# Natural row order and a new planned order in an adaLN, linear-attention and MLP kernel

## The chip, the cores and the metric

The kernel runs on one core of a Trainium2 chip. Its time is the device time of one execution in microseconds (us), and less is better. The core has TensorE (PE, matrix products; PEld is its weight loads), VectorE (DVE), ScalarE (ACT), GpSimd (POOL) and SyncE (SP). Each engine works off its own instructions in a fixed order and waits for the others by semaphores. In this part of the kernel all transfers are issued by SP, so SP's queue is also the queue of the transfers.

## What is computed (reference, cut)

```python
def _A_ref(x, wqkv, wo):                 # H = 32 heads of 18
    qkv = ...(x @ wqkv)...               # q, k, v
    phi = lambda t: jnp.where(t > 0, t + 1, jnp.exp(t)) + 1e-6
    pq, pk = phi(q), phi(k)
    kv = jnp.einsum("bhsd,bhse->bhde", pk, v)
    z = jnp.einsum("bhsd->bhd", pk)
    num = jnp.einsum("bhqd,bhde->bhqe", pq, kv)
    den = jnp.einsum("bhqd,bhd->bhq", pq, z)[..., None] + 1e-6
    return ...(num / den)... @ wo

def _B_ref(x, w1, w2):
    return _silu(x @ w1) @ w2

mod = (_silu(c) @ w_mod).reshape(c.shape[0], 6, 1, -1)
sa, ca, ga, sb, cb, gb = (mod[:, 0], ..., mod[:, 5])
h = _layernorm(x) * (1 + ca) + sa
x = x + ga * _A_ref(h, A_wqkv, A_wo)
h = _layernorm(x) * (1 + cb) + sb
x = x + gb * _B_ref(h, B_w1, B_w2)
```

x has 2048 rows (tokens) of 576; wqkv is 576 x 1728, w1 576 x 4608, w2 4608 x 576, w_mod 576 x 3456. All are float32.

## The kernel before, in words

**Tiles.** The rows are handled as 16 tiles of 128 (t = 0 to 15), four of them to a block (b = 0 to 3). `acc[t]` in `accb[b]` holds a tile's results. A float32 operand of a matmul is split into a high and a low part, and a product takes three passes, so each split is an ACT copy (high) and a DVE or POOL subtraction (low).

**Stages.** Up to about 35 us block 0 and the weights are started, in an order written by hand. From about 30 to 250 us runs the *planned stage*: k for tiles 2 to 15 and q for tiles 0 to 10 (L851), the sums of x against phi(k) (L971), the product with the v weights (L1099), and with Wo (L1136). After it come attention and the first MLP groups (to about 400 us), the MLP (L1826 up, L1910 down) and the last plain group (L1943), whose output is added by `plain_add` (L1948) and stored by `plain_store` (L1954).

**The planned stage's order.** `pe(...)` and `do(...)` enter steps with an engine, an assumed duration, what they read and write, and a lag (how long after a transfer is issued its data are assumed to land). `Schedule.emit` works out for each step the latest start (`late`) that does not delay PE's fixed order, then walks through time: each engine takes, of the steps that are ready, the one with the smallest `late`. The result is the fixed order on every engine, SP's queue included. A static order of this kind that assumes a landing too early puts a waiting instruction in front of others that could run.

**A block's turn.** `early_steps(b)` loads the block's four tiles into `accb[3]` (`row4`, L916), takes their statistics (DVE L242, L243) and works out mean and deviation (L923 DVE, L924 POOL, L925 DVE). `block_steps(b)` normalises (L257 ACT, L259 DVE), transposes 32 x 32 pieces on DVE (L936), stores them to DRAM (`turned`, L942) and fetches them back turned (L948, and the tail L953). `turn_steps(b)` modulates the fetched chunks (L265, L267) and splits them into `hT` (L907 ACT, L908 DVE), which PE's products with the k and q weights read. `dealt` and `taken` are views that reorder the columns as they are written to `hT`, so that column t*128 + p belongs to partition p of tile t.

**Row order before.** For t >= 4, `pieces` says where a tile's rows lie: partition 32a + j of tile t of a block holds row 128a + 32t + j. A load of a tile, of a block, or a store of a result is therefore four transfers of 32 partitions each (L916, L723, L1933, L1954).

**Projected tiles.** `phi_steps` takes exp on ACT (L857), the maximum on DVE (L862), and their combination on DVE (L407). A PSUM bank of the two (`K0`, `K1`) is free once exp and maximum have read it. `k_steps` then splits the tile (L872 ACT, L875 DVE or POOL) and adds it to `zsum` (POOL L876).

**Modulation sums and first scan.** `mod_steps(piece)` makes two of the six modulation vectors each: five loads of w_mod (L347) into two rooms, `raw2`, scaled on ACT (L1012, L1014), added on POOL (L1015), the partial sums written to DRAM (`parts`, L1016), read back in another order in 36-byte runs (L1019), reduced on DVE (L1022) and written out as a vector (L1023). Before, piece 1 stands in block 0 and piece 2 in block 1. `bound_steps` and `first_scan`/`factor_first` take maxima and sums of squares from which the MLP's scale factors come; they stand at the end of the stage. `load_late` loads Wo and the v weights and multiplies Wo by the gate (L1088, DVE).

Of the kernel before, what the change touches and what calls it, by code (L numbers as in the profile page):

```python
# [24 lines left out]
def kernel(ctx: ExitStack, tc, A_x, A_wqkv, A_wo, B_x, B_w1, B_w2, c, w_mod, out):  # L25
# [33 lines left out]
    def behind(instructions):  # L59

        with ExitStack() as order:
# [31 lines left out]
            2-4 0-1 6-13 5 14-25 28-31 26-27 32-43 50-53 47 45 44 46 55-62 49 54 48 63-66 68 67 70-71 69 74 83  # L93
            73 75-76 72 77-81 84-85 87 86 82
# [235 lines left out]

    def pieces(t, n=1):
        if t < 4:
            return [(slice(0, P), lambda y: y[t * P : (t + n) * P].rearrange("(u p) d -> p u d", u=n))]
        r0 = [t // 4 * 512 + a * P + t % 4 * 32 for a in range(4)]
        return [(slice(32 * a, 32 * a + 32), lambda y, r=r: y[r : r + 32 * n].rearrange("(u j) d -> j u d", u=n))
                for a, r in enumerate(r0)]
# [387 lines left out]

    def q_norm(t, prod, pn):
# [10 lines left out]
        load_rows_of(a, t)  # L736
        return pn

    class Schedule:
# [4 lines left out]
        def __init__(self):  # L744
            self.ops, self.wrote, self.seen, self.order = [], {}, {}, []

        def add(self, eng, us, emit, reads=(), writes=(), lag=0.0, tensor=None):
# [8 lines left out]
            self.ops.append((eng, us, emit, lag, need))  # L756
            if eng == "PE":
                self.order.append((tensor, i))

        def emit(self):  # L760
# [18 lines left out]
            turn = 0  # L779
            for _ in range(n):  # L780
# [8 lines left out]
                i = min((i for i in some if ready[i] <= at_), key=lambda i: (late[i], i))  # L789
                open_[e].remove(i)  # L790
# [24 lines left out]
    plan = Schedule()  # L815
# [8 lines left out]
    def do(eng, us, emit, reads=(), writes=(), lag=0.0):  # L824
        plan.add(eng, us, emit, reads, writes, lag)
# [39 lines left out]
    BY_ACT = ()  # L865
# [12 lines left out]
    def q_steps(t):  # L878
        ps, k = project(t, wqp_)
        phi_steps(ps, k, acc[t], [f"acc{t}", *ACC.get(t, ())])  # L880

    def split_rows():

        C = KC * P
        for t in range(4):
            do("ACT", 0.68, lambda t=t: A.copy(xs[t][:, :D], xt[:, t, :D]), [f"xt{t}"], [f"xhi{t}"])
            eng, us = (V, 0.74) if t < 2 else (G, 1.55)
            do("DVE" if t < 2 else "POOL", us, lambda t=t, eng=eng: eng.tensor_sub(xs[t][:, DX:], xt[:, t, :C], f32(xs[t][:, :C])),
# [9 lines left out]
    def turn_steps(b):  # L898

        for k in START:  # L900
# [3 lines left out]
            eng, us = (V, 0.69) if k in (1, 3) else (A, 0.81)  # L904
            do("DVE" if k in (1, 3) else "ACT", us, lambda src=src, chunk=chunk, eng=eng: modulate(src, *chunk[1:], eng), [], [name])
# [4 lines left out]
    def early_steps(b):  # L910
# [16 lines left out]
    def block_steps(b):  # L927

        row4 = accb[NB - 1]
        for t in range(4):  # L930
            eng, us = (A, 0.87) if t % 2 else (V, 0.7)
            do("ACT" if t % 2 else "DVE", us, lambda t=t, eng=eng: ln.normalise(t, xt[:, t], row4[:, t], eng, ((0, 0, D),)),
# [67 lines left out]
    raws2 = [[f"raw{i}.{a}" for a in range(2)] for i in range(2)]  # L1000
    of_raw = count()

    def mod_steps(piece):
        parts, vec = parts_of[piece - 1], vec_of[piece - 1]
        for k in START:
            kp, i = P if k < KC else 64, next(of_raw) % 2
            raw, dst = raw2[i], tmod2[:kp, :, 0:D]
            kp = raw.shape[0] if k < KC else 64
            do("SP", 0.1, lambda raw=raw, k=k: load_mod(raw, piece, k), [], raws2[i], 8.0)
            scale = sc[:kp, k : k + 1]  # L1010
            if k == 0:
                do("ACT", 1.25, lambda raw=raw, dst=dst, kp=kp, scale=scale: A.activation(dst, raw[:kp], AF.Identity, scale=scale), raws2[i], ["tmod"])  # L1012
            else:
                do("ACT", 1.25, lambda raw=raw, kp=kp, scale=scale: A.activation(raw[:kp], raw[:kp], AF.Identity, scale=scale), [], raws2[i])  # L1014
                do("POOL", 2.7, lambda raw=raw, dst=dst, kp=kp: G.tensor_add(dst, dst, raw[:kp]), raws2[i], ["tmod"])  # L1015
        do("SP", 0.1, lambda: nc.sync.dma_start(parts, tmod2[:, :, 0:D]), ["tmod"], [f"parts{piece}"], 5.5)  # L1016
# [3 lines left out]
           [f"parts{piece}"], raws2[i], 8.0)  # L1020
# [3 lines left out]
           [f"s9{piece}"], [f"vec{piece}"], 5.0)  # L1024
# [12 lines left out]
    first_spots = [r[:, i : i + n] for r in (sq, xT) for i, n in ((0, 1024), (1024, 1024), (2048, 256))]  # L1037

    def first_scan():
        parts, *n = scans(0, first_spots, 1024)  # L1040
        rooms = [SQ[0:2], SQ[2:3], SQ[3:4], XT[0:2], XT[2:4], ["xT4"]]
        for (load, square), room in zip(parts, rooms):
            do("SP", 0.1, load, [], room, 8.0)
# [1271 lines left out]
```

## Time and profile before

| | us |
|---|---|
| median of 3 runs | 1146.26 (1145.07 to 1146.29) |
| the profiled execution | 1145.7 |
| its span, first to last instruction | 1144.0 |
| mean granted TensorE clock | 0.976 of full speed |

| engine | busy us | share of the span |
|---|---|---|
| PE | 1081.1 | 95% |
| DVE | 927.1 | 81% |
| POOL | 722.1 | 63% |
| ACT | 695.5 | 61% |

Two views carry most of what follows. The busy time by stretch gives, for a piece of the span, how long each engine worked and at which clock PE ran. The timeline of an engine gives each instruction, or a run of equal ones, with its start and duration; in brackets behind it stand the idle time before it and what ended that. Rows named SPq are issues of transfers: their duration is that of the issue. The time from issue to landing stands in the view of the transfers, as the last number of a row.

### The profile page before, as it was taken

The page shows a single profiled execution, that of the slowest core. Times are in us where ns is not written, and L with a number is a line of the kernel's source. Part 1 is how long each engine was busy: PE and PEld are TensorE (multiplying, and loading weights), DVE is VectorE, ACT ScalarE, POOL GpSimd, SP SyncE. Part 2 cuts the span into 40 slices and gives each one's busy share as a digit, 9 for nine tenths or more (in the row PEclk, how much of TensorE's full clock was granted, in tenths as well). Part 3 has the DMA queues.
Part 4 walks back from the last instruction along what each step waited for, and adds up shares of the span by engine and source line. Part 5 has one row for each costly group of instructions (what it writes and reads, how often), then busy time and mean ns, then how long its engine had stood idle before and what let it go on. Part 6 is the DMA issues. An engine that isn't in the chain of part 4 may idle for free.

```text
span 1144.0 us, 19228 instructions
## 1 busy us (share of the span) xinstructions
PE 1081.1 (95%) x7027; PEld 773.8 (68%) x7027; DVE 927.1 (81%) x1467; ACT 695.5 (61%) x1300; POOL 722.1 (63%) x789
## 2 busy tenths in 40 slices
PE   8878797999999997999999999999999999999995
PEld 7878797899888544566666666666666666666664
DVE  7858494968699888989898888897897887898765
ACT  4653334333855668767777677686686586675562
POOL 2435162335462468977978868878778778777462
PEclk9988898899999999999999999999999999999998
DMA  9268629514333575767756757747748738626523
GB/s 287 60 160 100 154 68 144 152 54 110 120 85 129 207 230 164 268 165 235 218 182 219 213 171 241 228 135 253 230 117 256 235 111 272 200 78 196 163 72 83
DMA packets 121071, 193.52 MB, mean 169 GB/s; under 512 B 44492, under 2 KB 79312, under 8 KB 120976
## 3 DMA queue, kind: packets, MB, share of 16 engines
q1 hardware_dynamic: 120804, 192.00, 58.1%
q8 instruction: 55, 0.90, 0.3%
q10 hardware_dynamic: 172, 0.30, 0.1%
q14 instruction: 40, 0.33, 0.1%
HBM read 176.77 MB, written 15.48 MB: 168 GB/s over the span
## 4 chain that ended last, share of the span: by engine, by line
PE 73%; DVE 9%; DMA 7%; POOL 4%; ACT 3%; issue 2%; SPq 1%; DVEq 0%; POOLq 0%; ACTq 0%
PE up L1826 28%; PE down L1910 28%; PE big L295 7%; PE psK L851 3%; DMA acc<-turned 2%; PE small L1334 1%; PE psG L971 1%; DMA turned<-acc 1%; PE big L1345 1%; DMA raw<-parts 1%; DVE xt L259 1%; PE psK L1136 1%; DVE acc L936 1%; DVE a L407 1%; PE big L1259 1%
## 5 line engine op out<-in xcount | busy, mean ns | idle before, releaser
L1826 PE MATMUL up<-hT,w 128*128 128x512 f16 x1264 | 317.0, 380 | 8.2 <-DMA hT<-hd 3.2
L1826 PEld LDWEIGHTS <-w 128*128 128x128 f16 x1492 | 146.0, 98 | 142.5 <-issue 10.0
L1919 DVE SCALAR_TENSOR_TENSOR acc<-acc,set,down 128x576 f32<-128x576 f32 x128 | 103.5, 810 | 34.8 <-PE down L1910 33.9
L1864 POOL TENSOR_TENSOR s<-f,f 128x256 f32<-128x256 f32 x66 | 54.7, 830 | 92.5 <-ACT f L1845 90.2
L1844 ACT ACTIVATE f<-f,set 128x512 f32<-128x512 f32 x102 | 73.3, 719 | 61.5 <-DVE f L1850 51.6
L1910 PE MATMUL down<-w,hb 128*128 128x288 f16 x600 | 88.9, 286 | 2.5 <-DVE U L1921 1.7
L1910 PE MATMUL down<-w,hc 128*128 128x288 f16 x600 | 88.9, 286 | 0.2 <-DVE acc L1923 0.2
L1910 PE MATMUL down<-w,hT 128*128 128x288 f16 x480 | 82.9, 286 | 0.4 <-DVE acc L1923 0.4
L1848 DVE TENSOR_TENSOR f<-up,p 128x512 f32<-128x512 f32 x102 | 69.5, 682 | 13.0 <-PE up L1826 7.6
L1845 ACT ACTIVATE f<-f,set 128x512 f32<-128x512 f32 x102 | 73.6, 722 | 3.3
L1910 PEld LDWEIGHTS <-hb 128*128 128x128 f16 x600 | 58.7, 98 | 24.6 <-issue 2.8
L851 PE MATMUL psK<-w,hT 128*128 128x288 f32 x308 | 54.5, 330 | 20.4 <-DVE hT L908 9.2
L1910 PEld LDWEIGHTS <-hc 128*128 128x128 f16 x600 | 58.7, 98 | 21.9 <-issue 0.5
L1850 DVE TENSOR_TENSOR f<-up,f 128x512 f32<-128x512 f32 x68 | 46.8, 688 | 24.5 <-PE up L1826 23.8
L1888 POOL TENSOR_TENSOR hc<-s,hc 128x512 f16<-128x512 f32 x50 | 62.8, 1255 | 5.6 <-ACT hc L1884 5.6
L1910 PEld LDWEIGHTS <-hT 128*128 128x128 f16 x480 | 46.9, 98 | 26.7 <-issue 0.8
L851 PEld LDWEIGHTS psK<-w,hT 128*128 128x128 f32 x308 | 49.6, 218 | 22.5 <-DVE hT L908 10.5
L1868 POOL TENSOR_TENSOR f<-f,s 128x256 f32<-128x256 f32 x66 | 53.6, 812 | 16.5 <-DVE hb L1888 9.4
L1861 POOL TENSOR_TENSOR s<-f 128x256 f32<-128x256 f32 x66 | 56.3, 852 | 7.0 <-ACT f L1841 4.8
L1866 POOL TENSOR_TENSOR s<-s,f 128x256 f32<-128x256 f32 x66 | 56.9, 863 | 3.4
L1910 PE MATMUL down<-w,hd 128*128 128x288 f16 x396 | 54.9, 288 | 0.0
L1910 PE MATMUL down<-w,ha 128*128 128x288 f16 x396 | 54.4, 286 | 0.1
(398 smaller groups left out, 2807.4 us busy)
## 6 DMA issues: line engine op xcount, KB each, us to landing
hT<-hd SPq DMA_DIRECT2D x101, 640.0 KB, 5.0
hT<-hd SPq DMA_DIRECT2D x65, 512.0 KB, 3.9
hT<-in_B_w_dram SPq DMA_DIRECT2D x14, 576.0 KB, 4.7
hT<-in_B_w_dram SPq DMA_DIRECT2D x28, 256.0 KB, 5.6
raw<-in_B_w_dram SPq DMA_DIRECT2D x9, 576.0 KB, 6.4
v<-in_B_w_dram SPq DMA_DIRECT2D x9, 576.0 KB, 5.2
acc<-in_A_x_dram SPq DMA_DIRECT2D x16, 288.0 KB, 6.3
raw<-in_w_mod_dram SPq DMA_DIRECT2D x8, 576.0 KB, 5.0
```

The source lines that it names most:

```text
L295: T.matmul(ps, xpart(a), wpart(b), start=n == 0, stop=n == len(XW) - 1)
L851: T.matmul(o, part(a), w(b), start=c == 0 and m == 0, stop=c == KC and m == 1)
L1826: T.matmul(ps, left, right, start=first and m == 0, stop=m == len(seq) - 1, skip_group_check=True)
L1844: A.activation(f, f, AF.Silu, scale=factor(self.g, "inv"))
L1845: aside(A.activation(f, f, AF.Identity, scale=factor(self.g, "delta")))
L1848: V.tensor_add(f, self.bank[bank[1]], self.p1)
L1861: G.tensor_sub(self.s3, half(i, 0, 0), half(i, 0, 1))
L1864: G.tensor_add(self.s[:, 0:1], half(i, 0, 1), half(i, 1, 1))
L1866: G.tensor_sub(self.s[:, 1:2], self.s[:, 0:1], half(i, 0, 0))
L1888: eng.tensor_sub(t[:, :, 1, :], src, t[:, :, 0, :])
L1910: T.matmul(ps[:, p, :HALF], left[:, u, p * P : (p + 1) * P], right[:, v], start=n in (1, 5, 7, 6) and j == 0, stop=j == len(passes) - 1, s ...
L1919: V.scalar_tensor_tensor(dst, dst, factor(self.g, "ratio"), ps[:, :, :HALF], op0=ALU.mult, op1=ALU.add)
```

## The change

**Row order.** `pieces` and `load_rows_of` are gone: partition p of tile t holds row 128t + p everywhere. Each load of a tile or a block and each store is one transfer over 128 partitions. `dealt` and `taken` stay as they are. The hand-written order of SP behind the planned stage is the same one, renumbered for the smaller number of transfers.

**The planner.** `add` takes a `due` time, by which a step should have been done; it enters `late`. With `ahead`, an engine other than PE and SP may leave the step that it would take, and wait for a more urgent one that becomes ready before that step would end. The second planned stage (the MLP) keeps the plain rule.

**Assumed landings.** Block loads 7 to 9, store 5.2 to 6, fetches 5 and 6 to 6 and 7, w_mod loads 8 to 9, `parts` write 5.5 to 8 and read 8 to 14, scan loads 8 to 14.

**Work moved.** `mod_steps(2)`, the gate's row, `bound_steps`, `first_scan` and `factor_first` are entered right behind `mod_steps(1)`, in block 0, with due times. w_mod is loaded into four rooms (two of them in `accb[1]`), and the POOL addition is split into two halves. The scan uses `raw2` in pieces of 1152 columns, and `z` for its broadcast; the mask is made ahead of the last `split_rows`. The maximum of the k tiles goes from DVE to ACT (`BY_ACT = range(4)`: Relu and a bias pass). Wo is loaded into `raw2` and `xt[0]`, and its gate multiplication goes from DVE to POOL.

```diff
-    def load_rows_of(a, t):
-        for p, rows in pieces(t):
-            nc.sync.dma_start(a[p], rows(x)[:, 0])
...
-        load_rows_of(a, t)
+        nc.sync.dma_start(a, x[t * P : (t + 1) * P, :])
...
-        def emit(self):
+        def emit(self, ahead=False):
...
-                late[i] = min(begin.get(i, t + 8.0), end - lag - us)
+                late[i] = min(begin.get(i, t + 8.0), self.due[i] - us, end - lag - us)
...
+                if ahead and e not in ("PE", "SP"):
+                    end = at_ + ops[i][1]
+                    urgent = [j for j in some if ready[j] < end and late[j] < min(late[i], end - shift)]
+                    i = min(urgent, key=lambda j: (late[j], j), default=i)
+                    at_ = max(at_, ready[i])
+                if e == "PE":
+                    shift = max(shift, at_ - begin[i])
...
-    BY_ACT = ()
+    BY_ACT, Q_ACT, NORM_V, TURN_V, XS_V, WO_V = range(4), (), (0, 2), (1, 3), (0, 1), False
...
-        def load():
-            for p, rows in pieces(4 * b, 4):
-                nc.sync.dma_start(row4[p], rows(x))
-
-        do("SP", 0.3, load, [], SQ, 7.0)
+        rows = x[b * 512 : (b + 1) * 512, :].rearrange("(t p) d -> p t d", p=P)
+        do("SP", 0.1, lambda: nc.sync.dma_start(row4, rows), [], SQ, 9.0)
...
-        do("SP", 0.4, store, SQ, [f"turned{b}"], 5.2)
-        do("SP", 0.4, fetch_main, [f"turned{b}"], XT, 5.0)
-        do("SP", 0.4, fetch_tail, [f"turned{b}"], [XTAIL], 6.0)
+        do("SP", 0.4, store, SQ, [f"turned{b}"], 6.0)
+        do("SP", 0.4, fetch_main, [f"turned{b}"], XT, 6.0)
+        do("SP", 0.4, fetch_tail, [f"turned{b}"], [XTAIL], 7.0)
...
+    mod_rooms = [accb[1][:, 0:2], accb[1][:, 2:4], *raw2]
+    mod_names = [["acc4", "acc5"], ["acc6", "acc7"], *raws2]
...
-                do("POOL", 2.7, lambda raw=raw, dst=dst, kp=kp: G.tensor_add(dst, dst, raw[:kp]), raws2[i], ["tmod"])
+                for a in range(2):
+                    do("POOL", 1.45, lambda raw=raw, dst=dst, a=a: G.tensor_add(dst[:, a], dst[:, a], raw[:, a]), [names[a]], [f"tmod{a}"])
...
-           [f"parts{piece}"], raws2[i], 8.0)
+           [f"parts{piece}"], raws2[i], 14.0)
...
+            do("ACT", 1.35, lambda square=square: square(found), [], [*room, "found"], due=140.0)
...
-            do("DVE", 1.1, lambda cc=cc, n=n: V.tensor_mul(wos[cc][:n], wos[cc][:n], bc["ga"][:n]), ["bcga"], [wo_names[cc]])
+            do("DVE" if WO_V else "POOL", 1.1 if WO_V else 1.5, lambda cc=cc, n=n: (V if WO_V else G).tensor_mul(wos[cc][:n], wos[cc][:n], bc["ga"][:n]), ["bcga"], [wo_names[cc]])
...
     mod_steps(1)
+    mod_steps(2)
+    do("SP", 0.1, lambda: mod_row("ga", vec_of[0][0]), ["vec1"], ["bcga"], 5.0)
+    bound_steps()
+    steps = first_scan()
+    factor_first(steps)
     q_steps(2)
...
-        plan.emit()
+        plan.emit(AHEAD)
...
         def store(self, b, i, k):
-            for p, rows in pieces(4 * b + 2 * i, 2):
-                nc.sync.dma_start(rows(of[:, k * HALF : (k + 1) * HALF]), self.c(b, i, k)[p])
+            t0 = (4 * b + 2 * i) * P
+            dst = of[t0 : t0 + 2 * P, k * HALF : (k + 1) * HALF]
+            nc.sync.dma_start(dst.rearrange("(i p) d -> p i d", p=P), self.c(b, i, k))
...
-            for p, rows in pieces(a):
-                nc.sync.dma_start(rows(of[:, c])[:, 0], acc[a][p, c])
+            nc.sync.dma_start(of[a * P : (a + 1) * P, c], acc[a][:, c])
```

More of the change, by code (lines that the diff above doesn't have):

```diff
@@ L1057, in bound_steps @@
         do("DVE", 0.75, lambda: find_limit(2, bc["gb"]), ["bcgb"], ["limits"])
-        do("DVE", 1.6, find_bounds, [], ["limits", "colb", "bounds"])
+        do("DVE", 1.6, find_bounds, [], ["limits", "colb", "bounds"], due=140.0)
     def factor_first(steps):
@@ L1076, in rest @@
             V.tensor_scalar(bc["gb"], bc["gb"], factor(0, "gamma"), None, op0=ALU.mult)
-        do("DVE", 2.0, rest, [], ["small", "bcgb"])
-    wos = [xt[:, i, :D] for i in range(4)] + [raw2[1][:, 0, :]]
-    wo_names = [f"xt{i}" for i in range(4)] + ["raw1.0"]
-    wvs = [acc[12 + i] for i in range(4)] + [raw2[1][:, 1, :]]
+        do("DVE", 2.0, rest, [], ["small", "bcgb"], due=175.0)
+    wos = [raw2[i // 2][:, i % 2] for i in range(4)] + [xt[:, 0, :D]]
+    wo_names = [*raws2[0], *raws2[1], "xt0"]
+    wvs = [acc[12 + i] for i in range(4)] + [xt[:, 1, :D]]
     def load_late():
@@ L1223 @@
     z_steps()
-    do("POOL", 1.2, lambda: G.memset(kvm, 0.0), [], ["tmod", "kvm"])
+    do("POOL", 1.2, lambda: G.memset(kvm, 0.0), [], ["tmod0", "tmod1", "kvm"])
     for c in (2, 3, 4):
```

86 lines of the change are left out of this document (38 added, 48 removed).

## The prediction

> **What bounds the kernel now.** I began with the busy time of each engine by stage (start and end of a stretch in us, its length, then busy us and instruction count of PE, PEld, DVE, ACT and POOL, the granted TensorE clock, the DMA share, GB/s).
>
> ```profile
> 30.00:250.00 220.00, 188.59 (x1253) 181.69 (x1254) 160.44 (x247) 87.36 (x140) 82.47 (x57) 0.90 0.56 113
> 250.00:400.00 150.00, 146.48 (x1055) 125.02 (x1056) 126.51 (x230) 88.52 (x148) 75.32 (x71) 1.00 0.41 126
> 400.00:1100.00 700.00, 688.45 (x4338) 424.41 (x4336) 592.35 (x899) 486.73 (x960) 537.70 (x634) 1.00 0.63 197
> 1100.00:1144.00 44.00, 32.41 (x226) 21.88 (x224) 25.71 (x40) 17.65 (x27) 19.13 (x17) 0.93 0.29 75
> ```
>
> From 250 to 1100 TensorE is busy for 834.93 of 850 us at full clock, and the edits there concern only row loads that no PE wait names. So the change is worth what it does in two places: the planned stage (30 to 250 us: 31.4 us of PE idle, clock 0.90) and the end.
>
> In the planned stage I read PE's waits next (waiter, released by: us in total, times, longest), then the stretches around them.
>
> ```profile
> PE psK L851 <- DVE hT L908: 10.9, 5, 4.6
> PE psK L851 <- DVE a L862: 7.9, 2, 6.0
> PE psK L851 <- ACT hT L907: 5.1, 2, 3.0
> PE psG L971 <- DVE w L875: 4.3, 3, 3.1
> ...
> 58.00:78.00 20.00, 17.84 (x114) 17.84 (x115) 9.70 (x13) 7.46 (x12) 6.69 (x4) 0.83 0.74 185
> 78.00:92.00 14.00, 7.73 (x42) 6.68 (x42) 12.13 (x16) 6.95 (x11) 5.85 (x3) 0.81 0.40 99
> 124.00:138.00 14.00, 7.18 (x31) 6.39 (x31) 8.17 (x17) 7.21 (x12) 2.49 (x2) 0.63 0.75 180
> 149.00:164.00 15.00, 13.10 (x85) 12.68 (x84) 14.83 (x18) 5.22 (x7) 10.25 (x7) 0.89 0.08 21
> 180.00:191.00 11.00, 8.17 (x41) 8.17 (x42) 8.19 (x14) 8.81 (x15) 3.48 (x3) 0.69 0.83 167
> 191.00:210.00 19.00, 12.96 (x88) 12.73 (x87) 10.67 (x12) 8.92 (x19) 8.18 (x6) 0.82 1.31 210
> ...
> 278.95 7.46 PE big L295 x56
> ```
>
> The last row is the same matmul at full clock: 7.46 / 56 = 0.133 us each. A stretch's length less 0.133 times its matmuls is what it loses, idle and slow clock together: 4.8, 8.4, 9.9, 3.7, 5.5 and 7.3 us, in the order of the rows, 39.6 in all. A gap costs more than itself, because the matmuls behind it run slowly: 24 of them took 4.98 us after a gap of 1.90 and 3.35 without one.
>
> ```profile
> 151.12 4.98 PE L851 MATMUL psK<-wq,hT 128*128 128x288 f32 x24 [1.90 <-DVE a L862]
> ...
> 156.47 3.35 PE L851 MATMUL psK<-wq,hT 128*128 128x288 f32 x24
> ```
>
> **The end: one store for four.** PE and DVE are done at 1132.83 + 1.13 = 1133.96, but the 36 store issues of L1954 keep SP's queue busy to 1124.34 + 17.59 = 1141.93 (0.49 each), and the span ends at 1144.0, that is 2.07 us after the last issue has ended.
>
> ```profile
> 1132.83 1.13 DVE L1948 SCALAR_TENSOR_TENSOR acc<-up,set,acc 128x288 f32<-128x288 f32 x2
> 1124.34 17.59 SPq L1954 DMA_DIRECT2D out_dram<-acc  x36
> 1076.40 0.39 SPq L1933 DMA_DIRECT2D out_dram<-acc  x1
> out_dram<-acc SPq DMA_DIRECT2D x4, 288.0 KB, 2.4
> out_dram<-acc SPq DMA_DIRECT2D x8, 36.0 KB, 1.6
> ```
>
> Afterwards nine stores over 128 partitions stand there. One such issue takes 0.39 (the third row). Per tile that is under half a microsecond against some 3 us of matmuls, so the queue is empty when the last half tile is ready. It lands later than a 36 KB piece (1.6) and sooner than a 288 KB one (2.4); I take 0.4 more than now. New end: 1133.96 + 0.05 wait + 0.4 issue + 2.07 + 0.4 = 1136.9. **Term: -7.1 us** (-6.5 to -7.5). The row loads from 250 to 350 us lose the same share of issues beside full matmuls: 0.
>
> **The planned stage.** Its PE order stays; orders on DVE, ACT, POOL and SP are worked out anew from other costs, lags and due times. The trace of before cannot show the new orders, so each loss is bounded by zero and by what its stretch loses, and what lies between is chosen by the rows that name its cause.
>
> ```profile
> 54.88 4.57 DVE L259 TENSOR_SCALAR xt<-acc,mv 128x576 f32<-128x576 f32 x2
> 56.29 2.83 POOL L1015 TENSOR_TENSOR tmod<-tmod,raw 128x1152 f32<-128x1152 f32 x1
> 83.39 0.82 DVE L242 BATCH_NORM_STATS2 st<-acc 128x6 f32<-128x288 f32 x2 [1.49 <-DMA acc<-in_A_x_dram]
> 83.86 5.63 POOL L1015 TENSOR_TENSOR tmod<-tmod,raw 128x1152 f32<-128x1152 f32 x2 [5.57 <-ACT raw L1014]
> 84.37 2.65 DVE L908 TENSOR_TENSOR hT<-acc,hT 128x512 fp32r<-128x512 f32 x1
> 86.95 3.10 DVE L908 TENSOR_TENSOR hT<-h,hT 128x512 fp32r<-128x512 f32 x1
> 131.08 0.82 DVE L242 BATCH_NORM_STATS2 st<-acc 128x6 f32<-128x288 f32 x2 [4.06 <-DMA acc<-in_A_x_dram]
> 132.06 2.52 DVE L908 TENSOR_TENSOR hT<-acc,hT 128x512 fp32r<-128x512 f32 x3
> 200.13 2.20 DVE L1022 TENSOR_REDUCE crow<-raw 128x9 f32<-128x1152 f32 x1 [7.93 <-DMA raw<-parts]
> ```
>
> - *Row statistics behind their landing* (x load: assumed lag 7 to 9; fetches 5 and 6 to 6 and 7). DVE runs in order. At 81.9 and 127.0 it reached L242 before the rows had landed, with the hT splits that PE needs queued behind. The wait, the statistics and the aggregate cost 1.49 + 0.82 + 0.21 = 2.5 and 4.06 + 0.82 + 0.21 = 5.1 us. With the later landings assumed, and with `ahead` holding DVE for a split that is about to be ready, the splits come first; statistics late by a few us delay nobody for most of a block. With part of the slow clock: 4 of the 8.4 (between -5, if a transfer comes late there, and 8.4) and 6 of the 9.9 (0 to 9.9).
> - *Modulation sum 2 out of the last block.* At 192.2 DVE went idle for 7.93 us in front of L1022, whose read takes 12.7 us to land where 8 was assumed; the maximum that frees PE's bank (L862) stood behind it, which is the 6.0 us wait. Now both sums come in block 0 and the lag is 14. The step takes its five loads, the `parts` write and read and the broadcasts, and the eight loads of the first scan, in front of the turned stores and fetches of blocks 1 and 2 on SP's queue. At 191:210 I take 6.5 of 7.3 (3 to 7.3), and at 180:191, where the fetch then shares the queue with no scan loads, 2.5 of 5.5 (0 to 5.5).
> - *Maximum of the k tiles on ACT.* 14 operations of 0.75 leave DVE (10.5 us); ACT gets Relu and a bias pass each, about as long as its Exp (0.65): 14 x 1.3 = 18 us on an engine that is busy for 87.36 of 220. The bank is then freed after two ACT passes in a row, some 0.6 us later, covered by the second bank while a tile takes 28 x 0.133 = 3.7. At 149:164 I take 1.5 of 3.7 (0 to 3.7), at 58:78 1.5 of 4.8 (-2 to 4.8).
> - *Wo times gate on POOL.* Four of 1.33 and one of 0.74 leave DVE; POOL pays about 1.49 each (L876, the same shape), 7.5 us that nothing needs before 240: 0.
> - *What comes back.* The 16 half adds on POOL and the transfers of sum 2 and of the scan now meet blocks 1 and 2. I take +3 (0 to +8).
>
> ```profile
> L862 DVE TENSOR_SCALAR a<-psK 128x576 f32<-128x576 f32 x14 | 10.5, 749 | 8.7 <-ACT e L857 7.0 <-PE psK L851 1.7
> L857 ACT ACTIVATE e<-psK 128x576 f32<-128x576 f32 x25 | 16.2, 647 | 54.0 <-DVE acc L862 27.6 <-PE psK L851 13.6 <-DVE a L862 8.6
> L1088 DVE TENSOR_TENSOR xt<-xt,bc_ga 126x576 f32<-126x576 f32 x4 | 5.3, 1334 | 0.3 <-DMA xt<-in_A_wo_dram 0.3
> L876 POOL TENSOR_TENSOR zsum<-zsum,a 128x576 f32<-128x576 f32 x14 | 20.9, 1491 | 30.0 <-DVE a L407 18.0 <-DVE mv L923 9.7 <-DMA raw<-in_A_wo_dram 2.2
> ...
> 65.03 5.07 DMA turned<-acc
> 71.43 5.53 DMA acc<-turned
> ...
> 119.20 5.47 DMA acc<-turned
> ...
> parts<-tmod SPq DMA_DIRECT2D x2, 576.0 KB, 3.9
> raw<-parts SPq DMA_DIRECT2D x2, 576.0 KB, 12.7
> ```
>
> **Sum.** Stage: 4 + 6 + 6.5 + 2.5 + 1.5 + 1.5 - 3 = 19. From 210 on PE has no gap, and from 250 on little else than PE work sets the end, so the gain is carried through. The profiled execution took 1145.7 us (span 1144.0 and 1.7 around it): 1145.7 - 19 - 7.1 = 1119.6. The median of the three runs is 0.56 above that execution, hence 1120.
>
> The Trainium skill (TensorE: Matmul & The Clock Gate, section "What's actually happening") says that the clock is halved only after an idle window of about 3.4 us. The pair of rows at 151 and 156 disagrees: a gap of 1.90 was enough. By the rule the short gaps that I leave standing would cost no slow matmuls, an estimate of 6 us less (a third of the 20 lost us that remain), 1114; I go by the rows.
>
> **Rivals.**
> 1. *All gaps close* (the stretches' 39.6 less some 6 for a start at each turn): 1146.3 - 7.1 - 33.6 = 1106. For it: DVE, the fullest engine, is relieved most. Against it: a turn goes through DRAM and back whatever the order is.
> 2. *The round trip sets the turns.* By the chain of waits the fetches land at 77.0 and 124.7, about where PE runs dry; if the order brings them no earlier and more queued transfers make up for the statistics, only the 6.5 and the end remain: 1146.3 - 13.6 = 1133.
> 3. *POOL takes it back.* Where POOL works, DVE's operations stretch: 4.57 for two at 54.88, against 0.75 each for a TENSOR_SCALAR of that size, is 3.1 too much; 2.65 + 3.10 at 84.37, against 0.84 each at 132.06, is 4.1. If blocks 1 and 2 each meet both, 14.4 of the 19 are gone: 1134. For it: the adds are moved right there. Against: halves hold POOL for about 1.45 instead of 2.83.
> 4. *The new order is no better and only the end pays*: 1139.
> 5. *Slower.* SP waits in its queue for the `parts` write (3.9) before it can issue the read (12.7 us), and the store and the fetches of a block stand behind. If both sums fall in front of a turn, PE waits 2 x (16.6 + 1.6 of slow restart) = 36.4, and the 10 us at the two turns aren't gained: 1146.3 - 7.1 - 9 + 36.4 = 1167. One such meeting leaves it near 1143; slower begins where such delays together pass 26 us. For it: at 192 us DVE did wait for that read. Against: a turn's store and fetch fill 65.0 to 77.0, 12 of the 48 us from one landing to the next, and the sums aren't due before the middle of the stage.
>
> On rival 3, the Trainium skill (SBUF — State Buffer, section "SBUF: two separate sides") says that POOL and DVE take their shared port pair as a lock for a whole instruction. The stretched rows at 54.88 and 84.37 agree; by the rule alone, each POOL operation moved there can cost DVE its full length, and the change would tend to 1134.
>
> **How the numbers follow.** Forecast (1113 to 1127) 0.45; rival 1 0.13; rival 2 0.15; rival 3 0.13; rival 4 0.05; rival 5 0.07; no change 0.02, where a late sum just pays for the gains. About 0.2% (2.3 us) is what a measurement of this kernel can tell from no change. All but the last two are faster: 0.91, 0.02 and 0.07. The range 1109 to 1138 holds the forecast, rivals 2 and 3 and the upper edge of rival 1.
>
> **What would show it.** L1954 as nine issues, the last one beginning within 0.5 us of DVE's last operation. On DVE no wait for `acc<-in_A_x` in front of an hT split. L1022 run twice before about 130 us, with no wait over 2 us. No L862 on the k tiles. PE's idle time between 30 and 250 us down from 31 to some 17 us, and its clock above 0.93. What would prove it wrong: gaps at the turns as long as before, with `acc<-turned` as releaser (rival 2), with stretched DVE operations beside POOL (rival 3), or with the store of a turn issued late behind `raw<-parts` (rival 5).

## The result and the profile after

The changed kernel takes 1110.84 us (median of four runs, 1108.92 to 1113.29) against 1146.12 for the kernel before: the ratio is 0.9695, 95% interval 0.9673 to 0.9717. Run again beside other kernels, where 1109 to 1113 was expected, it took 1108.07 us (1107.03 to 1112.49), ratio 0.967, interval 0.9647 to 0.9692. The forecast was 1120 us: the sign and the order of the gain are right, and the gain is 35 us where 26 were expected. The first time lies in the range of 1109 to 1138 by less than 2 us, the second just below it, and both lie below the 1113 to 1127 that the forecast itself stood for. The profiled execution took 1113.29 us, the longest of its four; its span is 1111.6 us.

TensorE's work between the first projection and the attention is the same sequence in all these kernels, so it can be cut into steps at fixed matmuls instead of at fixed times: the projections of a block, then its sums (with them the wait for the next turn). These are the steps of the kernel before and then of the kernel after, by the same view as in the prediction (start and end, length, busy us and count of PE, PEld, DVE, ACT and POOL, granted clock, DMA share, GB/s): block 1, the sums up to the turn of block 2, block 2, block 3, and all that comes after the stage.

```profile
75.20:106.90 31.70, 25.43 (x170) 24.38 (x170) 26.26 (x40) 16.16 (x24) 17.69 (x11) 0.89 0.90 106
106.90:126.30 19.40, 15.63 (x114) 14.92 (x113) 11.96 (x16) 4.29 (x7) 1.41 (x1) 1.00 0.73 183
126.30:164.10 37.80, 31.25 (x196) 30.11 (x197) 30.36 (x43) 15.26 (x23) 21.80 (x13) 0.82 0.30 75
182.80:211.90 29.10, 23.03 (x140) 22.80 (x141) 19.72 (x26) 17.14 (x32) 11.66 (x8) 0.78 1.13 194
249.10:1144.00 894.90, 868.24 (x5621) 571.91 (x5619) 745.29 (x1168) 593.54 (x1134) 632.68 (x721) 0.99 0.58 179
```

```profile
30.00:250.00 220.00, 206.59 (x1455) 199.74 (x1454) 157.77 (x268) 115.07 (x182) 107.52 (x85) 0.97 0.58 126
74.80:98.60 23.80, 23.46 (x170) 22.54 (x170) 19.20 (x36) 19.01 (x29) 10.21 (x8) 1.00 1.15 158
98.60:121.80 23.20, 17.35 (x113) 16.42 (x112) 12.58 (x17) 6.20 (x9) 14.83 (x10) 0.93 0.71 190
121.80:149.60 27.80, 27.80 (x196) 27.66 (x197) 24.50 (x43) 19.07 (x31) 14.37 (x11) 0.94 0.87 103
165.30:185.00 19.70, 19.02 (x142) 18.67 (x141) 12.96 (x28) 16.75 (x30) 12.47 (x11) 1.00 0.50 165
223.90:1111.60 887.70, 868.13 (x5621) 571.92 (x5619) 744.97 (x1168) 593.64 (x1134) 631.36 (x721) 1.00 0.58 180
```

Block 1 is 7.9 us shorter, block 2 10.0, block 3 9.4, and in all three PE is now busy nearly from end to end. The step up to the turn of block 2 (S1 in the table below) is 3.8 us longer. Behind the stage 7.2 us went (894.9 to 887.7), on the same 868 us of PE.

The largest waits of PE that are left in the stage (waiter, releaser: total, times, longest) are these; the 10.9 us for DVE's part of `hT` and the 7.9 for the maximum are gone:

```profile
PE psG L965 <- DVE w L872: 4.1, 5, 1.1
PE psK L848 <- ACT hT L904: 2.6, 1, 2.6
PE psK L848 <- DVE a L396: 2.0, 1, 2.0
```

At the turns of blocks 1 and 2 the timeline of DVE has the order that was forecast: the hT splits (L905) come first, and the row statistics (L242) behind them find their rows landed. Whether this order is what pays is for the experiments. The two reductions of the modulation sums (L1021) stand below them.

```profile
82.12 0.68 DVE L905 TENSOR_TENSOR hT<-h,hT 128x512 fp32r<-128x512 f32 x1
84.18 0.81 DVE L242 BATCH_NORM_STATS2 st<-acc 128x6 f32<-128x288 f32 x2
...
125.36 0.68 DVE L905 TENSOR_TENSOR hT<-h,hT 128x512 fp32r<-128x512 f32 x1
125.96 0.81 DVE L242 BATCH_NORM_STATS2 st<-acc 128x6 f32<-128x288 f32 x2
...
94.84 2.36 DVE L1021 TENSOR_REDUCE crow<-raw 128x9 f32<-128x1152 f32 x1 [2.65 <-DMA raw<-parts]
146.00 2.33 DVE L1021 TENSOR_REDUCE crow<-raw 128x9 f32<-128x1152 f32 x1
```

PE's timeline shows where S1 became longer. It waits for splits of block 1's k tiles at the start of the step (1.32 + 1.06 + 0.84 = 3.2 us) and for the turn of block 2 at its end (2.63):

```profile
101.64 0.53 PE L965 MATMUL psG<-w,xs 128*128 128x288 f32 x2 [1.32 <-ACT w L869]
103.23 0.80 PE L965 MATMUL psG<-w,xs 128*128 128x288 f32 x4 [1.06 <-DVE w L872]
105.13 1.26 PE L965 MATMUL psG<-w,v 128*128 128x288 f32 x4 [0.84 <-DVE w L872]
121.80 4.54 PE L848 MATMUL psK<-w,hT 128*128 128x288 f32 x20 [2.63 <-ACT hT L904]
```

In the repeated profile the first three waits are as long (3.1 us), the one for the turn is 0.69, and S1 is 22.4 us all the same. On DVE those splits stand behind the first reduction, which waited 2.65 us for its read. That this wait is their cause is not shown: with natural rows alone S1 is 22.6 us, and there the reduction did not wait.

At the end, DVE's last operations and the nine store issues of the timeline finish together, DVE at 1107.66 + 1.13 = 1108.79 and SP at 1099.18 + 9.96 = 1109.14:

```profile
1107.66 1.13 DVE L1948 SCALAR_TENSOR_TENSOR acc<-up,set,acc 128x288 f32<-128x288 f32 x2
1099.18 9.96 SPq L1953 DMA_DIRECT2D out_dram<-acc  x9
```

### The profile page after: what moved, and what is told of

Read it like the earlier page. It is cut to its first block, busy times and chain, and to the rows that moved or that the text cites. A ratio compares the mean times of both kernels' runs of the same rounds, so it can differ in the third digit from the quotient of the medians.

```text
span 1111.6 us, 19115 instructions
## 1 busy us (share of the span) xinstructions
PE 1074.5 (97%) x7027; PEld 766.9 (69%) x7027; DVE 903.1 (81%) x1448; ACT 712.9 (64%) x1326; POOL 730.4 (66%) x802
## 4 chain that ended last, share of the span: by engine, by line
PE 75%; DVE 8%; DMA 6%; ACT 5%; POOL 3%; issue 2%; SPq 1%; ACTq 0%; DVEq 0%; POOLq 0%
PE up L1825 30%; PE down L1909 29%; PE big L295 7%; PE psK L848 2%; DMA raw<-parts 1%; PE small L1333 1%; DMA turned<-acc 1%; PE big L1344 1%; DMA acc<-turned 1%; PE psG L965 1%; DVE hT L167 1%; PE psK L1134 1%; DVE a L400 1%; PE big L1258 1%; PE small L280 1%
## 5 line engine op out<-in xcount | busy, mean ns | idle before, releaser
L1909 PEld LDWEIGHTS <-hT 128*128 128x128 f16 x480 | 47.0, 98 | 26.6 <-issue 0.8
L1867 POOL TENSOR_TENSOR f<-f,s 128x256 f32<-128x256 f32 x66 | 53.3, 807 | 16.5 <-DVE hb L1887 9.4
L965 PE MATMUL psG<-w,xs 128*128 128x288 f32 x336 | 51.5, 306 | 4.3 <-DVE w L872 1.4
L295 PE MATMUL big<-w,qT 128*128 128x288 f32 x352 | 53.3, 299 | 0.8 <-ACT qT L1260 0.8
```

What stands on the lines that cost most here:

```text
L295: T.matmul(ps, xpart(a), wpart(b), start=n == 0, stop=n == len(XW) - 1)
L965: T.matmul(ps[:, h, :HALF], l, pk[t][:, u, h * HALF : (h + 1) * HALF], start=t == 0 and m == 0, stop=t == 3 and m == len(left) - 1)
L1909: T.matmul(ps[:, p, :HALF], left[:, u, p * P : (p + 1) * P], right[:, v], start=n in (1, 5, 7, 6) and j == 0, stop=j == len(passes) - 1, s ...
```

## The experiments

Each ratio is to the kernel before run on the same chip, whose median was 1146.1 to 1147.0 us. This table cuts each profile at the same matmuls of its timeline (us): F the first projections; S0, S1, S2 the sums of a block up to the next turn's first projection; B1, B2, B3 the projections of a block; T from block 3's sums to the attention's first transposes; "stage" their total; "rest" the span behind them. "One lag" is the landing assumed for the read of the partial sums.

| kernel | median | ratio (95%) | F | S0 | B1 | S1 | B2 | S2 | B3 | T | stage | rest |
|---|---|---|---|---|---|---|---|---|---|---|---|---|
| before | 1146.12 | 1 | 22.6 | 21.0 | 31.7 | 19.4 | 37.8 | 18.7 | 29.1 | 37.2 | 217.5 | 894.8 |
| after | 1110.84 | 0.9695 (0.9673–0.9717) | 22.5 | 19.0 | 23.8 | 23.2 | 27.8 | 15.7 | 19.7 | 38.9 | 190.6 | 887.7 |
| after, again | 1108.07 | 0.967 (0.9647–0.9692) | 21.0 | 19.6 | 24.0 | 22.4 | 27.0 | 14.9 | 19.2 | 39.0 | 187.2 | 888.0 |
| stores in four | 1117.24 | 0.9746 (0.9733–0.9759) | 21.0 | 19.6 | 24.6 | 21.1 | 27.0 | 14.9 | 18.9 | 39.0 | 186.2 | 896.4 |
| old landings | 1109.8 | 0.9684 (0.9668–0.97) | 21.0 | 17.2 | 27.0 | 22.3 | 27.0 | 15.8 | 18.7 | 38.8 | 188.0 | 888.9 |
| no look ahead | 1108.6 | 0.9666 (0.9653–0.9679) | 22.6 | 16.0 | 30.9 | 16.5 | 27.7 | 16.7 | 18.7 | 38.9 | 187.8 | 888.0 |
| neither of the two | 1111.79 | 0.9699 (0.9683–0.9715) | 22.6 | 15.4 | 26.4 | 20.4 | 32.5 | 14.9 | 18.7 | 39.0 | 189.8 | 889.8 |
| k maximum on DVE | 1114.33 | 0.9719 (0.9699–0.9738) | 22.6 | 21.0 | 29.6 | 15.5 | 28.0 | 16.8 | 20.0 | 39.1 | 192.5 | 890.9 |
| second sum late | 1118.3 | 0.9755 (0.9735–0.9776) | 30.9 | 16.7 | 26.4 | 17.6 | 26.1 | 17.1 | 18.7 | 42.1 | 195.6 | 887.9 |
| first read held | 1121.96 | 0.9781 (0.9759–0.9802) | 33.0 | 14.9 | 32.5 | 21.1 | 26.1 | 14.9 | 18.7 | 39.0 | 200.2 | 890.0 |
| before, natural rows | 1130.95 | 0.9861 (0.9844–0.9878) | 22.5 | 19.8 | 25.0 | 22.6 | 34.9 | 18.2 | 29.2 | 37.2 | 209.5 | 887.7 |
| before, k maximum on ACT | 1141.03 | 0.9952 (0.9934–0.9969) | 21.0 | 15.7 | 34.1 | 20.1 | 41.3 | 14.9 | 23.8 | 42.9 | 213.8 | 895.0 |
| before, one lag | 1148.62 | 1.0019 (1.0001–1.0036) | 21.0 | 21.2 | 30.6 | 18.7 | 39.7 | 17.0 | 28.9 | 41.9 | 219.1 | 897.3 |
| before, these three | 1124.63 | 0.9806 (0.9784–0.9828) | 22.4 | 15.3 | 26.6 | 19.9 | 29.9 | 16.1 | 32.4 | 41.2 | 203.8 | 889.6 |

The two profiles of the kernel after differ by 3.4 us in the stage. So a single step is read to about 2 us here, and less than that only by the medians.

**Stores in four.**

```diff
-            nc.sync.dma_start(of[a * P : (a + 1) * P, c], acc[a][:, c])
+            for r in range(0, P, 32):
+                nc.sync.dma_start(of[a * P + r : a * P + r + 32, c], acc[a][r : r + 32, c])
```

> The kernel after, with each of the last nine stores split into four of 32 partitions, as before the change (36 issues of about 0.49 us instead of nine). Theory: the issues of the last stores set the end, and the whole term of the prediction is here: the issues run on for some 7 us after the last operation of DVE, 1111 + 7 = 1118 us (1117 to 1119), and the attention begins where it does in the kernel after (223.9 us). Rival: the single store merely moved the last work, and most of the end's gain came with the earlier stage: 1111 to 1112 us.

1117.24 us, as the theory said. The stage is that of the kernel after, and the rest is 896.4 us against 887.7 and 888.0 (887.7 to 890.9 in all kernels with nine stores at the end). DVE's last operation ends at 1102.69 + 1.13 = 1103.82, while the last group of issues in this kernel's timeline runs to 1099.68 + 12.14 = 1111.82, and the span ends at 1114.0:

```profile
1099.68 12.14 SPq L1954 DMA_DIRECT2D out_dram<-acc  x26
```

**Old landings, no look ahead, neither.**

```diff
-        do("SP", 0.1, lambda: nc.sync.dma_start(row4, rows), [], SQ, 9.0)
+        do("SP", 0.1, lambda: nc.sync.dma_start(row4, rows), [], SQ, 7.0)
...
-        do("SP", 0.4, store, SQ, [f"turned{b}"], 6.0)
-        do("SP", 0.4, fetch_main, [f"turned{b}"], XT, 6.0)
-        do("SP", 0.4, fetch_tail, [f"turned{b}"], [XTAIL], 7.0)
+        do("SP", 0.4, store, SQ, [f"turned{b}"], 5.2)
+        do("SP", 0.4, fetch_main, [f"turned{b}"], XT, 5.0)
+        do("SP", 0.4, fetch_tail, [f"turned{b}"], [XTAIL], 6.0)
```

```diff
-    plan, AHEAD = Schedule(), True
+    plan, AHEAD = Schedule(), False
```

The first diff by itself, the second by itself, and then both:

> The kernel after, with the landings assumed as before the change (x load 7, store 5.2, fetches 5 and 6 us instead of 9, 6, 6 and 7). Theory of the prediction: the late landings assumed are what puts the hT splits ahead of the row statistics, so DVE waits again for landed rows in front of the splits and 5 to 10 us come back: 1116 to 1121 us. Rival: the x load as one transfer and the look ahead keep the splits first by themselves: within 2 us of the kernel after, 1109 to 1113.

> The kernel after, planned without looking ahead (an engine no longer stays free for a more urgent operation that is about to be ready). In the order of blocks 1 and 2 a row statistic then stands in front of the last hT splits. Theory: each such place costs TensorE a wait of one statistic (0.8 us) and of the landing if that is late, 1 to 4 us in all: 1112 to 1115 us. Rival: the look ahead carries most of the gain at the two turns, and the 4 + 6 us that the prediction counted there come back: 1118 to 1121.

> The kernel after with both taken away, the look ahead and the later landings (each of them alone cost nothing). Theory: each of the two does the other's work, and without both the row statistics stand in front of the hT splits before their rows have landed: 6 to 10 us come back, 1116 to 1120 us. Rival: neither has part in the gain at the turns, since the rows are in place by the time DVE comes to them for another reason: 1107 to 1111.

1109.8 and 1108.6 us: neither alone costs anything. The first is its rival's time; without the look ahead the run fell below both of its ranges. With both taken away it is 1111.79, just above its rival's range. That lies inside the interval of the first run of the kernel after, and by the medians 3.7 us above the second. In the timeline of this last kernel a statistic does stand in front of the splits again at the turn of block 2, and it waits (2.21 us, where the kernel before waited 4.06):

```profile
118.76 0.82 DVE L242 BATCH_NORM_STATS2 st<-acc 128x6 f32<-128x288 f32 x2 [2.21 <-DMA acc<-in_A_x_dram]
119.74 4.01 DVE L905 TENSOR_TENSOR hT<-acc,hT 128x512 fp32r<-128x512 f32 x3
```

B2 shows the price, 32.5 against 27.0 to 27.8, and S0 and S1 are shorter by about as much. So the new order at the turns is there as predicted, but it carries little of the gain.

**The kernel before with natural rows alone.** The plan is untouched; a row load or store is one transfer instead of four, and SP's hand-written order behind the stage is renumbered to fit (not shown).

```diff
     def pieces(t, n=1):
-        if t < 4:
-            return [(slice(0, P), lambda y: y[t * P : (t + n) * P].rearrange("(u p) d -> p u d", u=n))]
-        r0 = [t // 4 * 512 + a * P + t % 4 * 32 for a in range(4)]
-        return [(slice(32 * a, 32 * a + 32), lambda y, r=r: y[r : r + 32 * n].rearrange("(u j) d -> j u d", u=n))
-                for a, r in enumerate(r0)]
+        return [(slice(0, P), lambda y: y[t * P : (t + n) * P].rearrange("(u p) d -> p u d", u=n))]
```

> The kernel before with the natural rows alone (each load and store of rows is one transfer instead of four; plan, orders and costs as before). Theory: only the end pays, 7.1 us: 1138 to 1140 us, and the attention begins 217 to 218 us after the first projection as in the kernel before. Rival: the one load of a block's rows lands sooner than the four did, and the two waits of DVE for landed rows (1.5 and 4.1 us, with what they cost TensorE 2.5 and 5.1) close with it: 1130 to 1134.

1130.95 us: the rival. The rest is 7.1 us shorter, as forecast for the end, and the stage 8.0 us with it: block 1 6.7 and block 2 2.9 shorter, S1 3.2 longer. DVE still has the order of the kernel before. In this kernel's timeline the first statistic at the turn of block 1 finds its rows without a wait (1.49 us before), and the one at the turn of block 2 waits 1.47 us (4.06 before). The row load, one issue of 0.43 us at 118.40, is in place at 125.48, 7.08 us later; in the kernel before, four issues from 121.84 on took 3.16 us and the statistic began at 131.08, 9.24 us later.

```profile
83.10 0.81 DVE L242 BATCH_NORM_STATS2 st<-acc 128x6 f32<-128x288 f32 x2
...
118.40 0.43 SPq L912 DMA_DIRECT2D acc<-in_A_x_dram  x1
125.48 0.82 DVE L242 BATCH_NORM_STATS2 st<-acc 128x6 f32<-128x288 f32 x2 [1.47 <-DMA acc<-in_A_x_dram]
...
193.72 2.21 DVE L1018 TENSOR_REDUCE crow<-raw 128x9 f32<-128x1152 f32 x1 [8.05 <-DMA raw<-parts]
```

Block 3 keeps its 29.2 us here, and the last row shows that the wait for the second sum is untouched.

**The maximum of the k tiles**, back on DVE in the kernel after, and on ACT in the kernel before:

```diff
-    BY_ACT, Q_ACT, NORM_V, TURN_V, XS_V, WO_V = range(4), (), (0, 2), (1, 3), (0, 1), False
+    BY_ACT, Q_ACT, NORM_V, TURN_V, XS_V, WO_V = (), (), (0, 2), (1, 3), (0, 1), False
```

```diff
-    BY_ACT = ()
+    BY_ACT = range(4)
```

> The kernel after, with the maximum of the k tiles back on DVE (14 operations of 0.75 us leave ACT's two passes). Theory of the prediction: the move was worth some 3 us of the stage, so 1112 to 1115 us. Rival: DVE is the engine that holds every queue of the stage up, and its relief is most of what the prediction did not count: 8 us or more come back, 1117 to 1121.

> The kernel before with the maximum of the k tiles on ACT alone (planned anew from the same costs). Theory: while the second sum and the late rows still hold DVE up, its relief by 10.5 us is worth at most what the prediction counted for it: 0 to 4 us less, 1142 to 1146. Rival: the relief of DVE is the main cause of the whole gain in the stage: 10 us or more, 1136 or less.

1114.33 us, as the theory said: the ratios lie 0.0024 and 0.0049 above those of the two runs of the kernel after, 2.8 and 5.6 us of 1147. Alone on the kernel before the move gives 1141.03, 6.0 us less by the medians, between theory and rival and nearer the theory. The move is worth the 3 us counted or somewhat more.

**The second sum late.** The loads of the second sum wait for the turn of block 2; the scan stays early.

```diff
-            i = next(of_raw) % 4
+            i = next(of_raw) % 4 if piece == 1 else 2 + k % 2
...
-            do("SP", 0.1, lambda room=room, k=k: load_mod(room, piece, k), [], names, 9.0)
+            do("SP", 0.1, lambda room=room, k=k: load_mod(room, piece, k), ["turned2"] if piece == 2 else [], names, 9.0)
...
-    mod_steps(2)
     do("SP", 0.1, lambda: mod_row("ga", vec_of[0][0]), ["vec1"], ["bcga"], 5.0)
-    bound_steps()
     steps = first_scan()
-    factor_first(steps)
...
         k_steps(t)
+    mod_steps(2)
     q_steps(4)
...
+    bound_steps()
     for c in START:
         sum_steps(2, c)
...
     load_late()
+    factor_first(steps)
     q_steps(8)
...
-           [f"parts{piece}"], raws2[i], 14.0)
+           [f"parts{piece}", XTAIL] if piece == 1 else [f"parts{piece}"], raws2[i], 14.0)
```

> The kernel after, with the second modulation sum, the bounds and the first factor back at the places in the program that they had before, and the loads of the second sum held until the turn of block 2; block 1's fetch of the tail and the parts write come ahead of the main fetch there. Theory: the reduction of the second sum stands on DVE in front of work that TensorE needs late in the stage again, and 6 to 9 us come back: 1117 to 1120 us, with the start of the attention at 230 to 233 us instead of 223.9. Rival: the lag of 14 us that the plan now assumes for the read keeps DVE clear wherever the sum stands: within 2 us of the kernel after.

1118.3 us is in the theory's range, and yet it is not the theory's evidence. Block 3, where the loss was to come back, takes 18.7 us against 19.7 and 19.2 in the kernel after, and the attention begins at 225.4 us, not at 230 to 233. The loss is in F, 30.9 us, before anything of the second sum is due. The timeline shows it there: the statistics of block 1's rows stand on DVE ahead of block 0's maximum (L859) that frees PE's bank, and PE waits 5.48 us.

```profile
43.11 0.77 DVE L242 BATCH_NORM_STATS2 st<-acc 128x6 f32<-128x288 f32 x2
...
44.23 0.75 DVE L859 TENSOR_SCALAR acc<-psK 128x576 f32<-128x576 f32 x1
...
45.04 4.75 PE L848 MATMUL psK<-w,hT 128*128 128x288 f32 x20 [5.48 <-DVE acc L859]
...
183.36 2.34 DVE L1021 TENSOR_REDUCE crow<-raw 128x9 f32<-128x1152 f32 x1 [4.16 <-DMA raw<-parts]
```

The last line of the diff does this. With the read of the first sum made to wait for block 1's tail fetch, that fetch, the turned store and the statistics before it inherit the sum's due time, and the plan calls them urgent. The last run below, which has both sums early and this same line (with 22 us), shows the same loss in F, 33.0 us. What the late sum itself costs is in the last row: DVE waits 4.16 us at the end of block 3, and T is 3.1 us longer.

**One lag in the kernel before, and three parts together.** First the landing of 14 us alone; then this with the natural rows and the maximum on ACT, both as above.

```diff
-           [f"parts{piece}"], raws2[i], 8.0)
+           [f"parts{piece}"], raws2[i], 14.0)
```

> The kernel before with one figure changed: the plan assumes that the read of the partial sums lands after 14 us instead of 8. The second sum stays in the last block; its parts write and read now come ahead of that block's scan loads. Theory: the misjudged landing alone caused the wait of 7.9 us on DVE in block 3, the step takes 9 to 10 us less (29.1 to about 20), and something of it is lost at the fetch that the parts write now precedes: 1137 to 1141 us. Rival: the read lands late wherever the plan puts it, since it meets the fetch and the scan loads, and only the move into block 0 helps: 1144 to 1148.

> The kernel before with three small parts of the change: natural rows, the landing of 14 us for that read, and the maximum of the k tiles on ACT. The sums, the scan, the half adds, the look ahead, the other landings and Wo stay as before. Theory: these three (16, about 8 and 6 us when alone) are most of the gain and add up with a loss of some 3 us: 1117 to 1123 us. Rival: the second sum and the scan a block earlier are what makes the rest possible, and the three together leave it at 1126 or more.

1148.62 us: just above the rival's range, and not for its reason. The wait that the prediction priced at 6.5 us has indeed gone from DVE (7.93 to 1.27 us), and block 3 takes 28.9 us all the same. The timeline of this kernel has ACT idle in front of the scan's passes (L650), for 6.24 + 0.63 + 1.99 = 8.9 us, behind SP's eight scan loads, which now stand behind the read. PE in its turn waits 4.21 us for the Exp (L857) that ACT has behind the first of these passes:

```profile
174.05 1.31 SPq L1019 DMA_DIRECT2D raw<-parts  x1
175.45 16.16 SPq L649 DMA_DIRECT2D acc<-in_B_w_dram  x8
...
189.63 2.20 DVE L1022 TENSOR_REDUCE crow<-raw 128x9 f32<-128x1152 f32 x1 [1.27 <-DMA raw<-parts]
...
191.58 1.06 ACT L650 ACTIVATE acc<-acc 128x1024 f32<-128x1024 f32 x1 [6.24 <-DMA acc<-in_B_w_dram]
193.89 1.06 ACT L650 ACTIVATE acc<-acc 128x1024 f32<-128x1024 f32 x1 [0.63 <-DMA acc<-in_B_w_dram]
197.42 1.06 ACT L650 ACTIVATE acc<-acc 128x1024 f32<-128x1024 f32 x1 [1.99 <-DMA acc<-in_B_w_dram]
193.32 4.44 PE L851 MATMUL psK<-w,hT 128*128 128x288 f32 x20 [4.21 <-ACT e L857]
```

The kernel before has the same wait of ACT beside that of DVE, from 194.5 to 201.7 us, where DVE waited from 192.2 to 200.1:

```profile
201.68 1.06 ACT L650 ACTIVATE acc<-acc 128x1024 f32<-128x1024 f32 x1 [7.15 <-DMA acc<-in_B_w_dram]
```

With the three parts together the time is 1124.63 us, between the two ranges. The steps up to S2 add up to 130.2 us, as in the kernel after (132.0 and 128.9), and block 3 is worse than before, 32.4 us. Its timeline has no wait on DVE in front of the reduction. ACT waits 8.90 us in front of a scan pass, and DVE 14.11 us for the load of Wo, which stands behind the scan loads on SP's queue. The combination (L403) behind Wo's product on DVE then holds ACT for another 4.43 us, and PE waits 12.01 us for the Exp that comes next on ACT. Of these waits the one for Wo ended last:

```profile
179.20 1.06 ACT L646 ACTIVATE acc<-acc 128x1024 f32<-128x1024 f32 x1 [8.90 <-DMA acc<-in_B_w_dram]
182.33 2.41 DVE L1084 TENSOR_TENSOR xt<-xt,bc_ga 126x576 f32<-126x576 f32 x3 [14.11 <-DMA xt<-in_A_wo_dram]
185.33 2.23 DVE L1018 TENSOR_REDUCE crow<-raw 128x9 f32<-128x1152 f32 x1
185.45 0.67 ACT L868 CAST w<-a 128x576 fp32r<-128x576 f32 x1 [4.43 <-DVE a L403]
187.26 4.95 PE L847 MATMUL psK<-wq,hT 128*128 128x288 f32 x24 [12.01 <-ACT e L853]
```

From 1124.63 to the kernel after it is 14 to 17 us, and B3 and T make up 15 of them (32.4 + 41.2 against 19.7 + 38.9 and 19.2 + 39.0): the two steps in which the second sum, the scan and Wo's product on DVE stand.

**The first read held.** A version meant to be faster than the kernel after. There the store of block 2's turn is issued at 105.55, behind the broadcasts of the first sum, although its transposes had ended at 100.26 + 1.43 = 101.69 (timelines of DVE and SP):

```profile
100.26 1.43 DVE L930 STREAM_TRANSPOSE acc<-xt 128x576 f32<-128x576 f32 x2
102.82 0.33 SPq L677 DMA_DIRECT2D bc_gb<-vec  x1
104.87 0.59 SPq L1033 DMA_DIRECT2D bc_ga<-vec  x1
105.55 3.86 SPq L936 DMA_DIRECT2D turned<-acc  x4
```

```diff
-           [f"parts{piece}"], raws2[i], 14.0)
+           [f"parts{piece}", XTAIL] if piece == 1 else [f"parts{piece}"], raws2[i], 22.0)
```

> The kernel after with the read of the first sum held until the fetch of block 1's tail and assumed to land after 22 us: block 2's turned store, fetch and row load then stand ahead of the broadcasts of the first sum on SP's queue, and the tail's fetch and the parts write ahead of block 1's main fetch. Theory: the store of block 2's turn no longer waits some 4 us behind the broadcasts, so the turn's gap closes: 3 to 5 us less than the kernel after, 1106 to 1108. Rival: block 1's main fetch comes later behind the tail and the parts write, and the first turn loses what the second gains: 1109 to 1114.

1121.96 us, worse than both. The store is now ahead of the broadcasts (87.98 against 101.16), and PE goes into block 2 without a wait, as the theory had it; but S1 still takes 21.1 us, for its waits at the start are there again. The loss is in F, 33.0 us, and B1, 32.5. In F the urgency passed back through the tail fetch puts the statistics ahead of the maximum, as above. In block 1 ACT waits 2.42 us for a load of w_mod in front of the tail's split, and PE 3.61 us for that split:

```profile
44.33 0.75 DVE L859 TENSOR_SCALAR acc<-psK 128x576 f32<-128x576 f32 x1
45.14 5.17 PE L848 MATMUL psK<-w,hT 128*128 128x288 f32 x20 [5.47 <-DVE acc L859]
85.92 1.25 ACT L1012 ACTIVATE raw<-raw,sc 64x1152 f32<-64x1152 f32 x1 [2.42 <-DMA raw<-in_w_mod_dram]
```

No version was found that beats the kernel after. Whether the scan's move alone would clear block 3 in the kernel before was not tried.

## Why the prediction was right, and by how much it was not

- **The end: right.** -7.1 was forecast; the rest shrank by 7.2 us, and with the stores back in four it grew by 8.4 to 8.7.
- **The stage: right in sign and place, too small.** The forecast was 19 us; the two profiles of the kernel after have 26.9 and 30.3. In the order of the table, with the forecast for the stretches that fall into a step: S0 2.0 and 1.4 (1.5); block 1 7.9 and 7.7 (4); block 2 10.0 and 10.8 (7.5); S2 with block 3 12.4 and 13.7 (9). Against these stand S1 and T, 5.5 and 4.8 us longer (3). F is as long as before in one profile and 1.5 shorter in the other, which no term had.
- **Which terms were mis-sized.** The prediction left about half of the loss at 78:92 and smaller parts elsewhere standing, as slow clock and as waits behind the first. Blocks 1 to 3 now run with PE busy for 23.46 of 23.8, 27.80 of 27.8 and 19.02 of 19.7 us. When the first wait went, so did the slow matmuls that it caused, and in these blocks no second wait stood behind it; new ones came in S1. Rival 1, all gaps closed at 1106, is nearer to the measured time than the forecast is, and had been given 0.13.
- **The cause at the turns: wrong.** "With the later landings assumed, and with `ahead` holding DVE for a split that is about to be ready, the splits come first" is what happens, but it is not what pays. Without both, the time rises by 1 to 4 us by the medians. The natural rows, which the prediction costed at nothing in the stage, took 6.7 us off block 1 and 2.9 off block 2 under the old order, 8.0 off the stage in all. There one load lands before DVE needs it at the first turn, and at the second DVE's wait falls from 4.06 to 1.47 us. The step that failed is the one that read the rows' change as an affair of the end alone. That the 10 us counted for these two turns came out at all, and with more, was luck: another part of the same change paid most of them.
- **Block 3: the right place, half the mechanism.** The prediction gave 6.5 us to the wait of DVE for the read and 2.5 to the queue. Removing DVE's wait alone gave nothing, because ACT stood idle for the scan loads in the same stretch, and each holds operations that free PE's banks. The trace of before shows ACT's 7.15 us there; the prediction priced only DVE's 7.93. With the scan early, even a late sum leaves block 3 at 18.7 us and costs T 3.1: the scan loads, counted at 2.5, look like a larger part than the sum. In that run Wo's product was on POOL as well. The prediction put this move at nothing, and with the three parts DVE waited 14.11 us for Wo's load; how block 3's gain divides between the scan and Wo stays open.
- **Parts that add up.** Natural rows took 16.0 us and the maximum on ACT 6.0; with one lag, which by itself gave nothing, the three took 22.3 together. The 14 to 17 us from there to the kernel after are what is left for all the other edits, and they fall on block 3 and T. The due times, the half adds and Wo on POOL had no run of their own.
- **Rivals.** The round trip (1133) does not set the turns: blocks 1 and 2 gained 7.9 and 10.0 us. POOL (1134) did not take it back: the last split takes 0.68 us at both turns, where 3.10 was seen at the first one before. The slower case had one trace of itself: the broadcasts of the first sum stand in front of the turned store at 105.55. PE's wait for that turn is 2.63 us in one profile and 0.69 in the other.
- **What would show it.** Nine issues, the last beginning about when DVE ends: seen. No wait for rows in front of a split: seen. PE idle 31 down to 17 and the clock above 0.93: 13.4 (220 - 206.59) and 0.97, of which the window's last 26 us lie behind the stage after the change; from step to step of the stage the idle time fell from 31.0 to 12.6 us. Both reductions before 130 us with no wait over 2 us: missed, the second is at 146.00 and the first waited 2.65 us.

## What to carry to other kernels

Where several engines stand idle in one stretch, the longest wait is not yet the price: taking away most of DVE's 7.9 us gave nothing while ACT waited 8.9 us beside it. Price a stretch by the wait that would be last once the first is gone. When the layout of a transfer changes, look at when it lands for every reader, not only at its issues: one load in place of four closed or shortened waits that a new order was credited with. And an experiment whose total agrees with the theory still has to show its loss in the step that the theory names; the late sum hit its range by a loss 120 us earlier.

## What the runs showed of the hardware

The same 24 matmuls behind the same gap ran at two speeds in two executions of the same kernel after (timelines, second projection of the stage). First the profile first shown, then the repeated one:

```profile
39.28 4.97 PE L848 MATMUL psK<-wq,hT 128*128 128x288 f32 x24 [2.01 <-DVE a L396]
```

```profile
37.15 3.47 PE L848 MATMUL psK<-wq,hT 128*128 128x288 f32 x24 [2.01 <-DVE a L396]
```

So the price of a short gap is not fixed: 1.5 us more or nothing for 2.01 us. The Trainium skill (TensorE: Matmul & The Clock Gate, section "What's actually happening") says that activity is watched in a window that runs free of the kernel, so that the point where the clock changes differs from run to run; these two rows agree. It puts the idle time that slows the clock at about 3.4 us, and the first of the two rows, like the gap of 1.90 us in the prediction, was slowed after less.

The read of the partial sums (576 KB) was in place 15.6 us after its issue in the kernel with one lag (174.05 to 189.63) and 16.45 us in the kernel after (78.39 to 94.84, the row of its issue below), where the page of the kernel before had 12.7: the 14 us that the plan assumes are no upper bound.

```profile
78.39 0.38 SPq L1018 DMA_DIRECT2D raw<-parts  x1
```
